# A written list of single operations, carried on to the end of token tile 1, and attention steps spread one at a time over tiles 2 and 3

## The chip, the cores and the metric

One Trainium2 chip, one core. The metric is the device time of one execution in microseconds (us). The kernel before took 558.62 us in the median of three runs (558.17 to 561.63).

## What is computed

The reference runs a chunked scan attention over 4 batches and 8 heads, 768 positions each, and feeds its output, 3072 tokens of 256 features, through two feed-forward networks:

```
for each chunk:                       # the kernel uses chunks of 96 positions, 8 of them
    cum = cumsum(log(clip(a)));  L = exp(cum_i - cum_j), causal
    y = ((C B^T) * L) x + exp(cum) * (C state)
    state = exp(sum) * state + sum_j B_j x_j exp(cum_end - cum_j)
h   = max(x w1, x w2, x w3)           # 256 -> 768
x   = h w_out                         # 768 -> 256
out = (sigmoid(x w_gate) * (x w_val)) w_out2      # 256 -> 1536 -> 256
```

All in float32. Products of the networks are made of three matmuls of split operands (high and low parts), and the weights arrive as 64-bit words that the kernel decodes to float32 and splits.

## The kernel before, in words

**Tiling.** The 3072 tokens are cut into six token tiles of 512. For a tile the first network has six slices m of 128 hidden features. A slice takes three groups of six matmuls (128x512) into three PSUM banks, one for each of w1, w2, w3; a copy and two maxima form the hidden slice s, a cast and a subtraction split it (hi, lo), and one group of six matmuls adds its share to the output banks. So a tile has 24 groups. The second network follows from about 281 us on.

**Attention.** It is cut into 64 steps; step k belongs to chunk c = k // 8 and to a group of four (batch, head) units. A step has a score (line 315, four products; float32 for steps 0 to 15, with masked C; later of bf16 parts, bi and cs), a weighting of the scores with the decay (weigh, line 337; matrix m), a small product for the states (states, line 331, on GpSimd) and an output product (outputs, line 348). After each four steps, high and low (lines 366, 370) write a split half chunk into the ring xt_hi, xt_lo, which the networks read, and turn (line 393) transposes the states for the next chunk. Decays come from a scan on VectorE (line 270), two for a pair of steps, in four buffers that load_decay (line 254) refills by DMA. For chunks from 2 on, B and C are loaded to one buffer bc, cast to bf16 three times with two subtractions between (parts 0, 1, 2), and scattered by 12 DMAs to bi and cs. Tile t needs the chunks that hold its tokens: tile 1 all steps below 24, tile 2 below 32, tile 3 below 44, tile 4 below 56.

**The list.** ORDER is a text of words, each one operation; in_order (line 674) emits them so that every engine, and each queue, runs its words in that order. The words that the text below uses:

- Ld, LB, LC, Lb, Lx, Lwa: loads of decays, of B and C for chunks 0 and 1, of bc for a later chunk, of x and states' inputs, of weight words.
- k: masked C (ScalarE). S, m, bx, y: score, weighting, states' product, output product of a step. D2a: a decay scan. H, X, T: high, low, turn of a half chunk.
- sg, raw, r (ScalarE), stt, add, hi, lo with a name such as a10: the decode of half a slice's weights. stt is a shift and an or.
- P, Q, Pd: cast, subtraction and scattering DMAs of a later chunk (P32: chunk 3, part 2).
- F, E, U, V, h, l, O: matmul group, copy, two maxima, cast, subtraction and output group of tile 0 (F21: slice 2, bank 1).
- I: idle products, matmuls whose result nobody reads; a bare I is 14 of them (IDLE0), I with a number is one.

ON_DVE names the words that run on VectorE instead of GpSimd. In the list before, F to O run over tile 0 and the steps go to 23 (SHARED); it ends with O4 on TensorE. From there on a loop (line 709) emits tiles 1 to 5, four slots for each slice, one after each of its three groups and one after the output group of the slice before. At the end of a slot, slot_end (line 699) starts attention steps until UNTIL's share for this slot is reached, and advances the generators: a step of tiles 2 and 3 is asked for its score in its slot, prepared (weighting, next decays, casts of the next chunk: prepare, line 402) two slots later and its output comes three slots later. In tiles 2 and 3 a loop of two starts steps in pairs. For k from SHARED on, even steps are weighted by a copy on ScalarE and a product on GpSimd (line 340), and the output products of four steps are issued together (line 352). The loop's instructions are put in order by a planner when the program is built; its position against the end of the list is not fixed by the list. After slice 0 of tile 4 the attention's memory is given up and the loads of the second network's weights follow (line 136); their decode starts with the eighth slot of that tile.

## Time and profile before

| | us |
|---|---|
| median of three runs | 558.62 |
| lowest, highest | 558.17, 561.63 |
| the profiled execution | 562.51 |
| its span, first to last instruction | 560.7 |
| TensorE busy in the span | 536.0 |
| VectorE, ScalarE, GpSimd busy | 389.1, 323.6, 114.9 |
| mean granted TensorE clock | 0.985 |

Engines are PE (TensorE matmul), PEld (its weight loads), DVE (VectorE), ACT (ScalarE), POOL (GpSimd) and SP (SyncE, which issues DMAs). Matmuls are pipelined: their listed duration (some 390 ns) is longer than the distance from one to the next, so the cost of a group is read from starts. Positions are us from the span's first instruction.

### The profile page before, as it was taken

How to read it: one execution, taken by the hardware profiler on the slowest of the kernel's cores; microseconds unless marked ns; L12 is line 12 of the kernel's file. 1: busy time of each engine (PE TensorE's matmuls, PEld its weight loads, DVE VectorE, ACT ScalarE, POOL GpSimd, SP SyncE). 2: the span in 40 equal slices, each digit the busy share in tenths (PEclk: the TensorE clock that was granted, in tenths of full speed). 3: DMA queues.
4: the chain of work that ended last, by engine and by line, in shares of the span. 5: the costliest groups of instructions: out<-in, count | busy, mean ns of one | idle time of the engine just before them, and what ended most of it. 6: DMA issues, size and time to landing. Idle time of an engine off the chain costs nothing.

```text
span 560.7 us, 7987 instructions
## 1 busy us (share of the span) xinstructions
PE 536.0 (96%) x2914; PEld 423.2 (75%) x2914; DVE 389.1 (69%) x656; ACT 323.6 (58%) x571; POOL 114.9 (20%) x153
## 2 busy tenths in 40 slices
...
PEclk9899998979999999999999999999999999999999
...
GB/s 220 294 355 137 211 127 287 154 189 149 158 204 113 91 1 321 54 1 145 60 97 0 1 1 2 0 1 75 1 0 2 0 2 75 1 0 1 0 1 76
DMA packets 33895, 50.53 MB, mean 90 GB/s; under 512 B 3392, under 2 KB 19904, under 8 KB 33856
## 3 DMA queue, kind: packets, MB, share of 16 engines
...
q8 instruction: 23, 0.38, 0.3%
q10 hardware_dynamic: 288, 0.39, 0.2%
q14 instruction: 16, 0.13, 0.1%
...
## 4 chain that ended last, share of the span: by engine, by line
PE 77%; DVE 9%; DMA 7%; ACT 2%; issue 2%; SPq 1%; POOL 1%; DVEq 0%; POOLq 0%; ACTq 0%
PE o L812 17%; PE uv L781 15%; PE ug L781 15%; PE u L428 7%; PE u L430 6%; PE u L429 6%; DMA dec<-ad 3%; DVE dec L273 3%; PE o L428 2%; PE o L429 2%; PE o L430 2%; PE y L355 2%; DMA cs<-parts 1%; PE s L322 1%; PE s L325 1%
## 5 line engine op out<-in xcount | busy, mean ns | idle before, releaser
L812 PE MATMUL o<-hi,w_d 128*128 128x512 f32 x288 | 97.6, 390 | 0.0
L428 PE MATMUL u<-xt_hi,w_a 128*128 128x512 f32 x216 | 88.5, 410 | 5.6 <-DVE s L510 2.2
L781 PE MATMUL ug<-xt_hi,w_g 128*128 128x512 f32 x252 | 91.5, 392 | 0.1
L781 PE MATMUL uv<-xt_hi,w_v 128*128 128x512 f32 x252 | 90.3, 390 | 0.0
L429 PE MATMUL u<-xt_lo,w_a 128*128 128x512 f32 x216 | 85.4, 395 | 0.0
L430 PE MATMUL u<-xt_hi,w_a 128*128 128x512 f32 x216 | 85.3, 395 | 0.0
L812 PEld LDWEIGHTS o<-hi,w_d 128*128 128x128 f32 x288 | 54.0, 188 | 11.3 <-ACT hi L855 0.2
L273 DVE TENSOR_TENSOR_SCAN dec<-dec,delta 128x388 f32<-128x388 f32 x64 | 58.5, 946 | 5.7 <-DMA dec<-ad 5.4
L856 DVE TENSOR_TENSOR lo<-y,hi 128x512 fp32r<-128x512 f32 x72 | 49.4, 687 | 16.5 <-ACT hi L855 15.6
L812 PE MATMUL o<-lo,w_d 128*128 128x512 f32 x144 | 56.4, 392 | 0.8 <-DVE lo L856 0.8
L781 PEld LDWEIGHTS ug<-xt_hi,w_g 128*128 128x128 f32 x252 | 47.3, 188 | 12.0 <-ACT ug L784 0.9
L781 PEld LDWEIGHTS uv<-xt_hi,w_v 128*128 128x128 f32 x252 | 47.3, 188 | 10.6 <-DVE y L852 0.8
L428 PEld LDWEIGHTS u<-xt_hi,w_a 128*128 128x128 f32 x216 | 41.3, 191 | 17.0 <-DVE s L510 2.4
L781 PE MATMUL ug<-xt_lo,w_g 128*128 128x512 f32 x126 | 49.1, 390 | 0.0
L781 PE MATMUL uv<-xt_lo,w_v 128*128 128x512 f32 x126 | 49.0, 389 | 0.0
L499 ACT CAST hi<-s 128x512 fp32r<-128x512 f32 x30 | 18.6, 620 | 52.1 <-DVE s L510 51.6
L430 PEld LDWEIGHTS u<-xt_hi,w_a 128*128 128x128 f32 x216 | 41.1, 190 | 9.1
L855 ACT CAST hi<-y 128x512 fp32r<-128x512 f32 x72 | 44.4, 619 | 5.7 <-DVE y L852 4.3
L429 PEld LDWEIGHTS u<-xt_lo,w_a 128*128 128x128 f32 x216 | 41.3, 191 | 7.9 <-DVE xt_lo L372 0.2
L852 DVE TENSOR_TENSOR y<-uv,y 128x512 f32<-128x512 f32 x36 | 24.7, 687 | 31.3 <-PE uv L781 31.2
L789 DVE TENSOR_TENSOR y<-ug,y 128x512 f32<-128x512 f32 x36 | 24.8, 689 | 24.4 <-ACT y L786 17.4
L786 ACT COPY sv<-uv 128x512 f32<-128x512 f32 x36 | 21.2, 588 | 33.5 <-PE uv L781 33.4
...
## 6 DMA issues: line engine op xcount, KB each, us to landing
...
```

What stands on the lines that cost most here:

```text
L273: dve.tensor_tensor_scan(out=f, data0=f, data1=delta.rearrange("p u w -> p (u w)"), initial=0.0, op0=ALU.mult, op1=ALU.add)
L428: pe.matmul(ps, wlo, a_hi(k), start=k == 0, stop=False)
L429: pe.matmul(ps, whi, a_lo(k), start=False, stop=False)
L430: pe.matmul(ps, whi, a_hi(k), start=False, stop=k == kn - 1)
L499: act.copy(hl[0], s)
L781: turn[0] = pe.matmul(ps, w, x, start=new and e == 0, stop=e == 2, skip_group_check=not new)
L786: evict[0] = act.copy(self.temp(1 if i == 6 else 2), ps)
L789: evict[1] = dve.tensor_tensor(out=self.t[k], in0=ps, in1=self.t[k], op=ALU.add)
L812: turn[0] = pe.matmul(acc2[t][d], w, x, start=n == 1 and e == 0, stop=n == M2 and e == 2)
L852: evict[1] = dve.tensor_tensor(out=g, in0=v, in1=g, op=ALU.mult)
L855: act.copy(hl[0], g)
L856: dve.tensor_tensor(out=hl[1], in0=g, in1=hl[0].bitcast(F32), op=ALU.subtract)
```

## The change

The list gets a new order from its first word on and goes on to the end of tile 1 (except that tile's last output group): F, E, U, V, h, l and O now carry slices 0 to b, where 6 to b are the slices of tile 1. Steps 24 to 31 are in it (LISTED = 32, which also takes the even ones among them back to VectorE), f0 is the copy of tile 0's output, and chunk 4's casts and scatters are in it. The loop starts with tile 2. UNTIL gives steps 32 to 47 to tile 2 and 48 to 63 to tile 3, over 23 slots instead of 19, and a step is started alone. The bare I, I13 and I14 are gone, and ON_DVE has other words. In the old list, lines are left out.

```diff
--- before.py
+++ after.py
@@ -42,37 +42,43 @@
 FIRST = 2 * NG
 MASKED = 8
 SHARED = 24
+LISTED = 32
 MTS = 8
 DECS = 4
-UNTIL = [12, 24, 36, 50, 64, 64, 64]
+UNTIL = [12, 24, 32, 48, 64, 64, 64]
 SLOT = {1: 0, 2: 1, 6: 3, 5: 4, 7: 6, 3: 2, 4: 5}
 WEIGHT = {1: 0, 2: 2, 3: 1, 4: 3, 5: 4, 6: 5, 7: 6}
 
 ORDER = """
-LB0 Lx00#0 I a clip Ld0 K delta I0 pk LC0 k3 k1 k4 clip0 Ld1 D0a astore k0 D0b S3 S0 k5 clip1 D1a
-D1b m3 k2 Lwa00#0 Lwa00 Lx00 bx1 LC1 S1 sga00 rawa00 stta00 bx2 ra00 I1 S4 k12 m0 Ld2 D2a Ld3 m1
-k7 m4 Lb2 S2 m2 I2 S5 S7 D2b D3a bx3 y3 D3b adda00 hia00 I3 I4 k10 P20 m5 k15 Lwa01#0 Lwa01 y2 bx0
-Ld4 y0 LB1 D4a m7 k6 S6 y1 Lx01#0 Lx01 D4b Q20 k9 S9 P21 Q21 k11 k8 m6 S8 m9 bx4 H00 S11 m8 X00
...
-X20 Pd30#3 Pd30#4 Pd30 U5 Pd32#0 Pd32 V5 Ld12 D12a Lx30#0 Lx30 h5 l5 O4 D12b Ld13 Lx40#0 Lx31#0
-Lx31 Ld14 Ld15 D13b T21 T20 D13a Lx40
+LB0 K Lwa00#0 a clip LC0 pk delta Lwa00 sga00 rawa00 stta00 Ld0 clip0 k6 Ld1 k2 k4 D0b S2 ra00 k5
+clip1 D1a m2 adda00 I0 astore hia00 Lb2 P20 k0 D0a k1 I1 I2 Lx00#0 Lx00 bx2 Q20 k3 D1b Ld2 D2b I3
+I4 I5 I6 LC1 S0 m0 S3 k7 bx3 m3 bx0 S1 m1 P21 Ld3 S5 m5 k9 I7 k8 D2a bx1 Lwa01#0 Lwa01 k13 k11 S7
+loa00 D3a D3b m7 Lx01#0 sga01 rawa01 S4 m4 S6 m6 y3 Q21 Lwa10#0 Lx01 bx4 stta01 ra01 y4 Ld4 D4a y0
+y2 y1 H00 X00 D4b I8 I9 Lwa10 bx7 sga10 rawa10 stta10 k14 I10 I11 LB1 I12 k10 adda01 Ld5 bx5 y5
+Lx10#0 Lx10 y7 bx6 y6 H01 Lwa11#0 Lwa11 D5b bx11 D5a S11 S10 m11 S9 ra10 S8 T00 bx10 m10 y11 y10
+adda10 Ld6 hia01 m9 bx9 y9 m8 hia10 bx8 y8 H10 Ld7 sga11 rawa11 X01 ra11 Lwa20#0 Lwa20 sga20 X10
+loa10 loa01 Lwa21#0 Lwa21 D7a rawa20 D6b S13 m13 F00 F01 stta11 adda11 E0 sga21 rawa21 U0 ra20
+Lwa30#0 Lwa30 stta20 stta21 Lx11#0 Lx11 F02 F10 hia11 loa11 ra21 k12 Lwa31#0 sga30 Lwa31 V0 F11
+F12 E1 D7b bx14 h0 adda20 bx15 S12 rawa30 U1 V1 Ld8 l0 hia20 Ld9 ra30 sga31 Lx20#0 Lx20 adda21
+stta30 D6a hia21 m12 Lwa41#0 loa20 rawa31 ra31 O0 stta31 loa21 Lwa40#0 Lwa40 adda30 hia30 F20
+loa30 adda31 F21 P22 k15 F22 T10 h1 D8a E2 U2 bx16 V2 Lwa41 sga41 Lwa50#0 Lwa50 sga40 S14 m14
+rawa40 ra40 stta40 l1 hia31 adda40 hia40 Pd21#0 S15 rawa41 loa31 F30 h2 bx12 E3 Pd22#0 Pd22 O1 T01
+bx13 D9a bx18 F31 Pd21#1 m15 y15 y13 Pd21#2 ra41 D8b bx17 sga50 l2 stta41 adda41 rawa50 ra50
+stta50 loa40 U3 hia41 y12 F32 O2 Pd20#0 Pd20#1 Pd20#2 Pd20#3 D9b V3 Pd20#4 F40 loa41 Pd20 E4 Pd21
+S19 m19 S17 m17 y14 Ld10 Lwa51#0 h3 S16 F41 m16 adda50 hia50 loa50 Lwa51 sga51 rawa51 D10a l3
+Lx21#0 Lx21 Ld11 Lx31#0 U4 S20 m20 ra51 F42 V4 h4 S18 m18 F50 E5 O3 S22 Lb3 stta51 S23 adda51
+hia51 bx19 y18 y16 D11a Ld12 D10b bx21 m22 loa51 y17 D11b m23 y19 H11 X11 F51 S21 P30 F52 l4 T11
+bx23 y23 Lx31 m21 bx22 H20 X20 y21 U5 bx20 y20 y22 H21 Lx30#0 X21 Q30 V5 h5 Lx30 Pd30#0 D12a bx24
+Lx41#0 Lx41 O4 D12b bx25 Pd30#1 Pd30#2 F60 T20 F61 P31 Q31 E6 U6 F62 V6 P32 l5 F70 E7 O5 f0 Pd30#3
+Ld13 Ld14 D13b D14a D13a F71 h6 F72 F80 l6 O6 U7 V7 F81 h7 l7 Pd30#4 Pd30 bx27 E8 Pd32#0 Pd31#0
+Pd31#1 Pd31#2 Pd31 Pd32 S27 m27 Lb4 U8 P40 F82 V8 S24 D14b Pd40#0 bx29 m24 Q40 F90 O7 h8 l8 F91
+S25 m25 E9 F92 U9 V9 S26 h9 l9 P41 Pd40#1 Pd40#2 Pd40#3 m26 O8 Ld15 D15a D15b bx26 Fa0 Ea S28 m28
+Fa1 S30 m30 bx30 Fa2 bx31 Pd40#4 Pd40 Ua Va Ld16 Ld17 Q41 P42 S29 m29 Fb0 Pd42#0 Pd42 S31 m31 T21
+Fb1 Eb Pd41#0 Pd41#1 Pd41#2 y27 Lx50#0 H30 X30 Ub bx28 y31 Fb2 Vb O9 Pd41 H31 X31 ha la Oa Lx40#0
+D17b Lx40 Ld18 D16b Ld19 hb T31 lb D16a Lx50 D17a T30
 """
 IDLE0 = 14
-ON_DVE = """loa10 loa11 adda21 adda30 adda31 adda41 Q30 l3""".split()
+ON_DVE = """Q20 loa10 adda20 adda21 loa21 adda40 l2 loa40 l5 l6 l7 l8""".split()
 
 
 class Pipe:
@@ -337,7 +343,7 @@
     def weigh(k):
 
         m, ps, dc = mt[k % MTS], scores.pop(k), factors(k)
-        if k >= SHARED and k % 2 == 0:
+        if k >= LISTED and k % 2 == 0:
             act.copy(m[:, :, 0:CH], ps[:, :, 0:CH])
             pool.tensor_tensor(out=m[:, :, 0:CH], in0=m[:, :, 0:CH], in1=dc[:, :, 1:LW],
                                op=ALU.mult)
@@ -441,8 +447,9 @@
         if m == mn - 1:
             pipe.add(finish(t, acc[t]))
 
-    def finish1(t, ps):
-        yield
+    def finish1(t, ps, wait=True):
+        if wait:
+            yield
         for d in range(KD):
             act.copy(y1[:, d, t * TT:(t + 1) * TT], ps[d])
 
@@ -588,30 +595,29 @@
                 wt1[m] = [(v[:, 0, b], v[:, 1, b]) for v in (wts[f"a{m}0"], wts[f"a{m}1"])
                           for b in range(4)]
 
-    def first_layer(kind, m, j):
+    def token_tile(kind, t, m, j):
 
         if kind == "F":
             if j == 0:
-                s = tmpp.tile([128, TT], F32, tag="s", bufs=3, name=f"s3_0_{m}")
-                hidden_of[m] = s, [tmpp.tile([128, TT], F32R, tag=h, name=f"{h}3_0_{m}")
-                                   for h in ("hi", "lo")]
-            banks_of[m, j] = ps = psu.tile([128, TT], F32, tag="up", name=f"u3_0_{m}_{j}")
-            w = wts[f"a{m}{j // 2}"]
+                s = tmpp.tile([128, TT], F32, tag="s", bufs=3, name=f"s3_{t}_{m}")
+                hidden_of[t, m] = s, [tmpp.tile([128, TT], F32R, tag=h, name=f"{h}3_{t}_{m}")
+                                      for h in ("hi", "lo")]
+            banks_of[t, m, j] = ps = psu.tile([128, TT], F32, tag="up", name=f"u3_{t}_{m}_{j}")
+            w, o = wts[f"a{m}{j // 2}"], t * TT
             three(ps, range(KD), KD, [(w[:, 0, b], w[:, 1, b]) for b in range(4)], lambda k: KD * (j % 2) + k,
-                  lambda k: xt_hi[:, k, 0:TT], lambda k: xt_lo[:, k, 0:TT])
+                  lambda k: xt_hi[:, k, o:o + TT], lambda k: xt_lo[:, k, o:o + TT])
             return
+        s, hl = hidden_of[t, m]
         if kind == "O":
-            down(0, m, M1, wt1[m], hidden_of[m][1], finish1)
-            return
-        s, hl = hidden_of[m]
-        if kind == "E":
-            evict[0] = act.copy(s, banks_of[m, 0])
+            down(t, m, M1, wt1[m], hl, lambda t, ps: iter(()))
+        elif kind == "E":
+            evict[0] = act.copy(s, banks_of[t, m, 0])
         elif kind in "UV":
-            evict[1] = dve.tensor_tensor(out=s, in0=banks_of[m, 1 + (kind == "V")], in1=s, op=ALU.max)
+            evict[1] = dve.tensor_tensor(out=s, in0=banks_of[t, m, 1 + (kind == "V")], in1=s, op=ALU.max)
         elif kind == "h":
             act.copy(hl[0], s)
         else:
-            (dve if f"l{m}" in ON_DVE else pool).tensor_tensor(
+            (dve if kind + "0123456789abcdef"[M1 * t + m] in ON_DVE else pool).tensor_tensor(
                 out=hl[1], in0=s, in1=hl[0].bitcast(F32), op=ALU.subtract)
 
     def clip(t):
@@ -638,6 +644,8 @@
             else:
                 (dve if word in ON_DVE else pool).tensor_tensor(out=r, in0=r, in1=parts[:, p],
                                                                 op=ALU.subtract)
+        elif word == "f0":
+            next(finish1(0, acc[0], False), None)
         elif word == "pk":
             sp.dma_start(out=pk, in_=pick)
         elif word == "a":
@@ -655,7 +663,7 @@
         elif word[:-3] in ("sg", "raw", "r", "stt", "add", "hi", "lo") and word[-3] == "a":
             weight(word[:-3], word[-3:])
         elif word[0] in "FOEUVhl":
-            first_layer(word[0], int(word[1]), int(word[2:] or 0))
+            token_tile(word[0], *divmod(int(word[1], 16), M1), int(word[2:] or 0))
         elif word[0] in "HXT":
             {"H": high, "X": low, "T": turn}[word[0]](int(word[1]), int(word[2]))
         else:
@@ -688,25 +696,25 @@
                 tails[i.engine] = i
 
     in_order(ORDER)
-    done[0] = SHARED
+    done[0] = LISTED
 
 
     slots = 4 * M1
-    slot = slots
+    slot = 2 * slots
     wp2, wq, hlp, psx = [], [], [], []
-    pend = (0, M1 - 1, M1, wt1[M1 - 1], hidden_of[M1 - 1][1], finish1)
+    pend = (1, M1 - 1, M1, wt1[M1 - 1], hidden_of[1, M1 - 1][1], finish1)
 
     def slot_end():
         t, s = divmod(slot, slots)
         if t + 1 < NTT:
-            goal = UNTIL[t] + (UNTIL[t + 1] - UNTIL[t]) * (s + 1) / (slots - 5)
+            goal = UNTIL[t] + (UNTIL[t + 1] - UNTIL[t]) * (s + 1) / (slots - 1)
             while done[0] < min(goal, UNTIL[t + 1]):
-                for _ in range(2 if t > 1 else 1):
+                for _ in range(1):
                     att_step(1 if t > 1 else 0)
         tick()
         weights_tick(t < NTT - 2 or s % 4 == 3)
 
-    for t in range(1, NTT):
+    for t in range(2, NTT):
         for m in range(M1):
             for hl in layer(t, m, wt1[m], 3, most):
                 slot_end()
```

## Rows read from the trace of the kernel before

**Rows 1.** The page, 40 slices of the span: the granted clock in tenths.
```profile
PEclk9899998979999999999999999999999999999999
```
**Rows 2.** Busy time by stretch: PE, PEld, DVE, ACT, POOL, then clock, DMA share, GB/s.
```profile
0.00:34.60 34.60, 27.90 (x229) 19.61 (x229) 21.88 (x36) 20.52 (x36) 15.82 (x35) 0.90 0.85 272
34.60:82.00 47.40, 42.87 (x294) 31.53 (x294) 45.34 (x70) 33.55 (x56) 29.70 (x31) 1.00 0.86 188
82.00:133.30 51.30, 44.20 (x289) 32.64 (x289) 32.36 (x58) 17.61 (x30) 25.24 (x32) 0.90 0.92 215
133.30:216.50 83.20, 81.69 (x626) 62.25 (x625) 54.80 (x91) 30.99 (x57) 42.81 (x54) 1.00 0.52 118
216.50:281.10 64.60, 64.60 (x287) 53.49 (x286) 51.29 (x103) 43.73 (x78) 1.29 (x1) 1.00 0.31 108
281.10:560.70 279.60, 274.75 (x1199) 223.73 (x1197) 183.44 (x302) 177.22 (x318) 0.00 (x0) 1.00 0.04 16
```
**Rows 3.** The chain that ended last, one piece: start, us, what.
```profile
283.95 1.36 PE ug L781 x6
```
**Rows 4.** Waits of PE, 82 to 133.3 us: in total, times, longest.
```profile
PE s L325 <- DMA dec<-ad: 4.1, 1, 4.1
PE u L428 <- DVE s L510: 2.2, 1, 2.2
```
**Rows 5.** Timeline of PE around step 32: start, us, instruction, idle time before it.
```profile
107.91 0.97 PE L355 MATMUL y<-mt,xs 128*32 128x112 f32 x30
113.01 0.48 PE L325 MATMUL s<-cs,bi 96*128 96x96 bf16 x4 [4.14 <-DMA dec<-ad]
```
**Rows 6.** Busy time by stretch, two stretches at the lower clock.
```profile
22.50:29.40 6.90, 6.80 (x28) 5.67 (x28) 5.67 (x13) 4.13 (x7) 4.03 (x8) 0.51 0.90 279
...
111.30:118.10 6.80, 5.09 (x16) 3.47 (x17) 1.53 (x4) 2.21 (x4) 2.84 (x2) 0.50 0.59 199
```
**Rows 7.** Timeline of PE: a lone score between groups; a y block and two scores.
```profile
104.70 0.48 PE L428 MATMUL u<-xt_hi,w_a 128*128 128x512 f32 x1
...
106.19 0.34 PE L325 MATMUL s<-cs,bi 96*128 96x96 bf16 x4
106.36 0.48 PE L428 MATMUL u<-xt_hi,w_a 128*128 128x512 f32 x1
...
163.99 0.97 PE L355 MATMUL y<-mt,xs 128*32 128x112 f32 x32
164.89 0.52 PE L325 MATMUL s<-cs,bi 96*128 96x96 bf16 x8
165.23 0.71 PE L428 MATMUL o<-hi,w_a 128*128 128x512 f32 x2
```
**Rows 8.** Groups of DVE, 34.6 to 82 us: busy us, mean ns, idle before.
```profile
L576 DVE SCALAR_TENSOR_TENSOR t_a<-raw_a,sg 128x512 int32<-128x512 int32 x10 | 8.9, 887 | 0.2 <-ACT raw_a L570 0.2
...
L579 DVE CUSTOM_DVE_ANT_0 r_a<-t_a,r_a 128x1024 uint16<-128x1024 uint16 x4 | 3.1, 788 | 0.1
L585 DVE TENSOR_TENSOR w_a<-r_a,w_a 128x512 fp32r<-128x512 f32 x2 | 2.5, 1229 | 0.0
...
L639 DVE TENSOR_TENSOR bc<-bc,parts 128x896 f32<-128x896 f32 x1 | 1.2, 1183 | 0.0
```
**Rows 9.** Timeline of ACT: the last cast of chunk 4's B and C.
```profile
103.73 0.94 ACT L296 CAST parts<-bc 128x896 bf16<-128x896 f32 x1 [1.15 <-POOL bc L300]
```
**Rows 10.** Timeline of PE in the start: idle products and scores.
```profile
1.78 4.99 PE L670 MATMUL idle<-sg 128*128 128x512 bf16 x14 [1.78 <-POOL sg L156]
...
10.44 2.02 PE L322 MATMUL s<-y 128*128 128x96 f32 x16 [0.39 <-ACT y L311]
...
22.60 5.41 PE L322 MATMUL s<-y 128*128 128x96 f32 x24 [1.03 <-DMA y<-in_bch]
```
**Rows 11.** Timeline of SP's queue: decay load 4, and the second network's first weights.
```profile
16.24 0.33 SPq L257 DMA_DIRECT2D dec<-ad  x1
...
211.07 0.38 SPq L136 DMA_DIRECT2D raw_g<-in_wg  x1
```

More of the change, by code (lines that the diff above doesn't have):

```diff
@@ L51 @@
 ORDER = """
-LB0 Lx00#0 I a clip Ld0 K delta I0 pk LC0 k3 k1 k4 clip0 Ld1 D0a astore k0 D0b S3 S0 k5 clip1 D1a
-D1b m3 k2 Lwa00#0 Lwa00 Lx00 bx1 LC1 S1 sga00 rawa00 stta00 bx2 ra00 I1 S4 k12 m0 Ld2 D2a Ld3 m1
-k7 m4 Lb2 S2 m2 I2 S5 S7 D2b D3a bx3 y3 D3b adda00 hia00 I3 I4 k10 P20 m5 k15 Lwa01#0 Lwa01 y2 bx0
-Ld4 y0 LB1 D4a m7 k6 S6 y1 Lx01#0 Lx01 D4b Q20 k9 S9 P21 Q21 k11 k8 m6 S8 m9 bx4 H00 S11 m8 X00
-sga01 rawa01 stta01 ra01 Lx10#0 bx6 Lx10 T00 bx7 Lwa11#0 bx5 bx9 I5 I6 adda01 I7 I8 k14 y4 y7 Ld5
@@ L57 @@
-I9 I10 I11 D5b m11 y6 bx8 P22 hia01 I12 Lwa11 sga11 I13 k13 Ld6 D5a S10 m10 bx11 bx10 y8 y5 H01 y9
-y11 X01 y10 H10 X10 Lwa10#0 Lwa10 D6a sga10 rawa10 Ld7 loa00 ra10 rawa11 ra11 loa01 stta10 D7b S15
-m15 F00 F01 E0 Lwa20#0 Lwa20 sga20 U0 Lwa21#0 Lwa21 S13 adda10 hia10 stta11 adda11 loa10 rawa20
-ra20 stta20 D6b m13 F02 Ld8 V0 sga21 hia11 rawa21 stta21 F10 E1 F11 Lwa30#0 Lwa30 I14 Ld9 adda20
-hia20 loa11 h0 sga30 rawa30 F12 U1 S12 loa20 F20 Lwa31#0 Lx11#0 Lx11 bx15 D9a stta30 l0 ra21
-adda21 ra30 adda30 m12 O0 hia21 loa21 Lwa41#0 bx13 V1 bx12 D7a Lwa31 hia30 sga31 rawa31 stta31
@@ L69 @@
-Pd30#0 m18 D11a O3 F50 E5 bx21 S22 y18 stta51 S20 adda51 m22 S23 F51 D11b Pd31#0 Pd31#1 hia51 y16
-bx23 T11 Pd30#1 P32 y21 Pd30#2 bx22 y22 Pd31#2 m23 loa51 y23 l4 y19 m20 y20 H21 X21 H20 F52 Pd31
-X20 Pd30#3 Pd30#4 Pd30 U5 Pd32#0 Pd32 V5 Ld12 D12a Lx30#0 Lx30 h5 l5 O4 D12b Ld13 Lx40#0 Lx31#0
-Lx31 Ld14 Ld15 D13b T21 T20 D13a Lx40
+LB0 K Lwa00#0 a clip LC0 pk delta Lwa00 sga00 rawa00 stta00 Ld0 clip0 k6 Ld1 k2 k4 D0b S2 ra00 k5
+clip1 D1a m2 adda00 I0 astore hia00 Lb2 P20 k0 D0a k1 I1 I2 Lx00#0 Lx00 bx2 Q20 k3 D1b Ld2 D2b I3
@@ new lines @@
+I4 I5 I6 LC1 S0 m0 S3 k7 bx3 m3 bx0 S1 m1 P21 Ld3 S5 m5 k9 I7 k8 D2a bx1 Lwa01#0 Lwa01 k13 k11 S7
+loa00 D3a D3b m7 Lx01#0 sga01 rawa01 S4 m4 S6 m6 y3 Q21 Lwa10#0 Lx01 bx4 stta01 ra01 y4 Ld4 D4a y0
+y2 y1 H00 X00 D4b I8 I9 Lwa10 bx7 sga10 rawa10 stta10 k14 I10 I11 LB1 I12 k10 adda01 Ld5 bx5 y5
+Lx10#0 Lx10 y7 bx6 y6 H01 Lwa11#0 Lwa11 D5b bx11 D5a S11 S10 m11 S9 ra10 S8 T00 bx10 m10 y11 y10
+adda10 Ld6 hia01 m9 bx9 y9 m8 hia10 bx8 y8 H10 Ld7 sga11 rawa11 X01 ra11 Lwa20#0 Lwa20 sga20 X10
+loa10 loa01 Lwa21#0 Lwa21 D7a rawa20 D6b S13 m13 F00 F01 stta11 adda11 E0 sga21 rawa21 U0 ra20
```

22 lines of the change are left out of this document (16 added, 6 removed).

## The prediction

> **What bounds the kernel now.** I read the page first, then the stages, then the waits of the slow stage. The slices show TensorE (PE) at 9 of 10 from slice 9 on, with dips before that, and the granted clock below 1.00 in four groups of slices, all in the first 120 us [rows 1]. The table by stage puts limits to this [rows 2]. From 216.5 us to the end PE is busy for all but 4.8 of 344 us at clock 1.00: nothing in that part can give much, and anything that brings its start forward brings the end forward by as much. What can be won lies in the first 216 us, which fall into four stretches. I cut them by the matmuls of the list: the start up to F00 (34.6 us), the list's token tile 0 up to the end of O4 (82.0), the loop's tile 1 up to the end of O4 of that tile (133.3), and tiles 2 and 3 (216.5).
>
> A group of six 128x512 matmuls costs 1.36 us when nothing stands between them [rows 3]. A tile has 24 such groups, 32.6 us. Tile 1 took 51.3 us for them and 12 attention steps, with 44.2 us of PE busy and a mean clock of 0.90 [rows 2]. The waits there name two holes of 4.1 and 2.2 us [rows 4]. The first is the score of step 32: PE stood from the y block at 107.91 to 113.01 [rows 5]. The row names a decay load, but a score reads only bi and cs, so I put it down to the last scattered parts of chunk 4, issued just ahead of that load on the same queue. Behind the hole the clock fell: from 111.3 to 118.1 us it was 0.50 [rows 6], the 1.2 GHz level, and the 5.1 us of work from 113.0 to 118.1 gave away half, 2.5 us. So one such late score costs 4.1 + 2.5 = 6.6 us. The second hole is a max on VectorE (DVE) queued behind scans and transposes.
>
> In tile 0 the picture differs: DVE is busy 45.3 of 47.4 us [rows 2]. That stretch is DVE's, not PE's.
>
> **Tile 1 in the list.** After the change, tile 1 has its 24 groups (F60 to Fb2, O5 to Oa) in a hand-ordered row, and eight steps (24 to 31) with it, where it had twelve. No score of chunk 4 is left in it: S32 now comes with tile 2. In the list P42, the last cast of chunk 4, stands six groups, two y blocks and a score ahead of S32. The price of a lone score: from one group's start at 104.70 to the next at 106.36 are 1.66 us, 0.30 more than 1.36 [rows 3, 7]. A y block of four steps took 0.90 us, 163.99 to 164.89 [rows 7], about 1.04 with the same 0.13 us that a group after an interruption takes longer. Sum: 24 x 1.36 + 8 x 0.30 + 2 x 1.04 = 37.1 us, and 0.9 us that I allow for small waits: 38.0 against 51.3, **13.3 us less**. Bounds: no wait at all gives 14.2 less; both old holes with their clock, 8.8 more, gives 5.4 less.
>
> DVE can bear it. The even steps 24 to 30 now multiply scores on DVE (about 0.5 us each) instead of ScalarE and GpSimd (POOL), and l5 to l8 move to DVE; but in 82.0 to 133.3 DVE was busy only 32.4 of 51.3 us [rows 2], so some 6 us more find room.
>
> **Tile 0 in its new order.** PE's groups there are the same; DVE sets the length, so I count what DVE runs between X10 and V5. Scans (12), score products (12), maxima (12) and transposes (three sets) stay. It loses one shift-or of 0.89 us (stta10 goes ahead of F00), one of four weight additions (0.79) and Q30 (1.18), and gains one w_a subtraction (1.23) [rows 8]; the single l stays (l2 for l3). Sum: **1.6 us less**. The other orders I cost at nothing since DVE has no idle time to be closed beyond 2.1 us. Bounds: those means hold outliers (the shift-or's mean of 0.89 comes from runs of 0.68 and some near 1.8), so I allow 5 less if these vanish, and 3 more if the new order meets as many waits as it has unknown edges.
>
> **The start.** The 14 idle products that open the queue go (and I13, I14), and weight a00 is loaded and decoded first. On ScalarE (ACT) that puts its decode and P20, the first cast of chunk 2, ahead of masks k0, k1, k3, k7. P20's load is now issued before decay loads 2 and 3, so it should be there in time. By ACT's queue (three decode steps, three masks, a fourth mask, the hi cast, P20) S0 comes at about 15.5 us, where S0 and S1 ran from 10.44 [rows 10]. Behind S0 stand m0 and m1, which free the buffer that decay load 4 needs: its issue at 16.24 [rows 11] goes to about 19.3, and LB1, queued behind it on SP, goes with it. So scans and scores of chunk 1 start some 3 us later. DVE was busy for only 21.9 of the first 34.6 us [rows 2], waiting for scores between its scans, so I let it take up two of the three. F00 comes **1.0 us later**; bounds: 1.5 earlier (the weight's decode, now out of the way, is all gain) and 5.6 later (below).
>
> Removing the idle products changes the clock's history. The 14 took 4.99 us [rows 10], 0.36 each, where a matmul of as many columns takes 0.23 at full clock (1.36 / 6, [rows 3]): the first of them ran at the lower level. Three scores in the stretch at 0.51 took 5.41 us, two at full clock 2.02 [rows 6, 10]: a score costs 0.8 us more at 1.2 GHz. In the new list S2 and seven idle products run back to back ahead of S0, so I expect the upper level by S0. Beside this stands the Trainium skill ("TensorE: Matmul & The Clock Gate", "Part 1: The HAM clock gate"): throttled is the default, and only sustained activity lifts it. By that rule the scores behind S0 could still run throttled, and the sum would be -2.3 us instead of -6.9; it is the second rival, whose price below comes from rows. By the rows, the old list's fillers did lift the clock, so the trace agrees with the rule as far as it goes.
>
> **Tiles 2 and 3.** They now take 32 steps instead of 28, singly. Two scores together take 0.34 us, 164.89 to 165.23 [rows 7], and 0.13 behind them: 0.47 against 0.60 for two lone ones, 14 x 0.13 = 1.8 us. Four more steps are 4 x 0.30 + 1.04 = 2.2. **4.0 us more.** Then the even pace. Chunk 5's last cast P2 comes with step 35's preparation, about slot 6 of tile 2, and S40 is asked for at slot 11: five slots of 83.2 / 48 = 1.73 us [rows 2], 8.7 us. In the old tile 1, cast at 103.73 to score at 113.01 were 9.3 us [rows 5, 9]. So S40, and S56 likewise in tile 3, come a little late: I take 1.5 us each, **3.0**, bounds 0 and 13.2 (6.6 each). S48 has seven slots and is free of this.
>
> The attention's last y block slips from before tile 4 into its first slots. The first load of the second network's weights waits for it: it was issued at 211.07 [rows 11], 5.4 us before tile 4, and would come about 2.5 us into it. The decode starts after the eighth slot, 8 x 1.36 = 10.9 us in, so a load that lands within 8 us costs nothing. Without that cover ACT would stall on it, and with it the maxima and PE.
>
> **Sum**: -13.3 - 1.6 + 1.0 + 4.0 + 3.0 = **-6.9 us**. The profiled execution took 562.5 us with a span of 560.7, so it would give 555.6. It lies 3.9 us above the median of the three timed runs, 558.6; taken from that, **551.7 us**.
>
> **Rivals.**
> *More is won* (the new tile 0 loses 5 and S40, S56 are ready): 6.4 better, 545.3. For: DVE's outliers are there to be lost. Against: DVE is full in both orders.
> *A cold start*: were the seven scores S0 to S6 all at 1.2 GHz and passed on whole, F00 would come 5.6 us later instead of 1.0: 556.3. Seven scores at 0.8 are those 5.6. For: 22.5 to 29.4 us ran at 0.51 even with the fillers [rows 6]. Against: the dense run of S2 and I0 to I6.
> *One or two chunk boundaries as bad as S32 was*: with one at 6.6, 556.8; with both, 561.9.
> *Slower*: S48 too, so three boundaries at 6.6 instead of 3.0 in all: 568.5. It decides once the way from P2's cast to the next chunk's first score exceeds the slots between them by some 4 us. For: 9.3 against 8.7 us at two of them, and PE stood at S32 from 108.9 on. Against: in 133.3 to 216.5, with two such boundaries, PE was idle for only 1.5 of 83.2 us [rows 2].
> *The order does not hold*: the end of the list may be overtaken by the loop's instructions; then tile 1 keeps its holes, and the rest is about even: 558.6.
>
> **How the numbers follow.** Likeliest, 0.52: 551.7, own range 547.5 to 555.5, four fifths of it under 553.0. More won 0.13, cold start 0.12, one or two boundaries 0.09, order lost 0.04, three boundaries 0.10. Faster by over 1% (about what a measurement of this kernel can tell from no change) is under 553.0: 0.42 + 0.13 = 0.55. Within 1%: 0.10 + 0.12 + 0.09 + 0.04 = 0.35. Slower: 0.10. The range 545.0 to 562.0 leaves out three boundaries and half of "more won".
>
> **What would show it.** Right: tile 1's 24 groups within 37 to 40 us, no hole over 1 us and clock 1.00 in it; F00 at 34 to 37 us and O4's end at 79 to 84; tiles 2 and 3 at 86 to 92; the stretch from tile 4 on unchanged near 344 us. Wrong: a PE wait of 3 us or more at the scores of steps 32, 40 or 56 with clock 0.50 behind it; F00 past 38 us; O4 past 86, which would mean that the new order starves DVE; or waits of ACT for the second network's weights in tile 4.

## The result and the profile after

The changed kernel took 553.98 us (median of four runs, 552.49 to 554.9) where the kernel before, run beside it, took 558.96: a ratio of 0.9894 [0.9859, 0.9929]. Timed again later, beside other kernels, it took 554.14 us against 560.80, a ratio of 0.987 [0.9837, 0.9902]. So it is faster by 1.1 to 1.3%, some 5.0 to 6.7 us. 551.7 us had been forecast.

The profiled execution took 554.9 us with a span of 553.1. By stretch, cut at F00, at the first group of each tile and at the start of tile 4, and in the last row of the second fence the one stretch at half clock (columns: PE, PEld, DVE, ACT, POOL busy, then clock, DMA share, GB/s). The first fence is the row of clocks of the page.

```profile
PEclk9899999999999999999999999999999999999999
```
```profile
0.00:35.20 35.20, 22.35 (x213) 18.08 (x214) 24.02 (x38) 20.45 (x36) 15.20 (x35) 0.95 0.78 251
35.20:79.40 44.20, 42.11 (x293) 31.23 (x293) 42.27 (x68) 31.41 (x54) 29.22 (x30) 1.00 0.81 215
79.40:122.30 42.90, 38.31 (x248) 29.45 (x247) 29.83 (x52) 14.48 (x23) 11.99 (x15) 1.00 0.79 162
122.30:207.90 85.60, 83.02 (x636) 61.48 (x635) 60.69 (x103) 33.23 (x59) 49.64 (x65) 1.00 0.71 145
207.90:273.60 65.70, 65.70 (x319) 54.12 (x318) 53.13 (x105) 44.54 (x80) 1.27 (x1) 1.00 0.37 128
...
20.00:23.40 3.40, 3.40 (x17) 3.30 (x17) 2.81 (x5) 2.61 (x5) 2.20 (x3) 0.50 0.89 217
```

Set beside [rows 2], the start is 0.6 us longer, tile 0 is 3.2 us shorter, tile 1 8.4 us shorter, tiles 2 and 3 are 2.4 us longer and tile 4's stretch is 1.1 us longer (the last y block, 32 matmuls, has moved into it: x319 for x287). The sum is 7.6 us, from a span of 560.7 to 553.1. [rows 1] has three slices below 9 (not four groups, as I had read it); one is left. The record of the clock begins with its first rise, 5.5 us into the profile of before and 13.1 into this one; what ran ahead of that counts as full in these rows and in the mean clocks below.

The waits of PE in tile 1, and then in tiles 2 and 3 (total, times, longest), answer [rows 4]:

```profile
PE s L331 <- DMA cs<-parts: 2.6, 1, 2.6
PE s L331 <- DMA bc<-in_bch: 0.8, 1, 0.8
PE o L435 <- DVE lo L620: 0.7, 1, 0.7
...
PE s L331 <- DMA bc<-in_bch: 1.1, 1, 1.1
PE u L434 <- DVE s L517: 0.8, 2, 0.4
PE s L331 <- DVE s L517: 0.7, 1, 0.7
```

With one of 0.5 us that is left out, they come to 4.6 us in tile 1 and 2.6 in tiles 2 and 3. So a hole at step 32 is left, at 120.41. Its chain can be read across four engines (timelines of POOL, ACT, SP's queue and PE: start, us, instruction, idle time before it):

```profile
107.92 1.91 POOL L645 TENSOR_TENSOR bc<-bc,parts 128x896 f32<-128x896 f32 x1
...
104.14 0.93 ACT L643 CAST parts<-bc 128x896 bf16<-128x896 f32 x1
...
109.86 0.94 ACT L643 CAST parts<-bc 128x896 bf16<-128x896 f32 x1 [3.45 <-POOL bc L645]
...
110.83 0.56 SPq L638 DMA_DIRECT2D bi<-parts  x1
...
114.02 0.59 SPq L270 DMA_DIRECT2D xs<-in_xh  x1
114.66 0.55 SPq L638 DMA_DIRECT2D cs<-parts  x1
...
117.46 0.39 PE L434 MATMUL u<-xt_hi,w_a 128*128 128x512 f32 x1
120.41 0.33 PE L331 MATMUL s<-cs,bi 96*128 96x96 bf16 x4 [2.56 <-DMA cs<-parts]
120.56 0.71 PE L434 MATMUL o<-hi,w_a 128*128 128x512 f32 x2
```

The subtraction Q41 ran on POOL at 107.92, the last cast P42 at 109.86, and the last scattered part was issued at 114.66, behind five other scatters and a load of xs; the score came 5.7 us after that issue. By the list's order the first two of the six scatters (Pd42) carry part 2 and the last four (Pd41) carry part 1, which P41 had cast at 104.14: they stood on the queue behind Pd42, which waited for P42. So the part that came last had been cast over 9 us before its last scatter was issued; no run put Pd41 ahead of Pd42. From cast to score it is 10.6 us, where the old tile 1 had 9.3 [rows 5, 9]. Unlike in [rows 6], no half clock follows the hole.

**How much of the gain is the clock.** The profiled execution of before, at a mean clock of 0.985, was one of its slower ones. Over 71 timed runs of the kernel before, its mean clock was 0.990 and its mean span 558.8 us; over ten runs of the changed one, 0.9976 and 552.1. Since half clock is one of two levels, 0.010 and 0.0024 below full mean 11.3 and 2.7 us at half clock in an execution, 8.6 us less, of which up to half, 4.3 us, is work not done. The kernel before alone gives a smaller slope: its 15 runs at 0.985 and 0.986 have a mean span of 560.2 us, its six at 0.997 have 556.2, 4.0 us for 0.011 of the clock, and by that slope the 0.0077 between the two kernels are worth 2.7 us. At a clock of 0.997 the changed kernel's two runs have 552.4. So of a mean gain of 6.7 us in span some 3.8 to 4.0 are there at one clock, and the rest is time at half clock that the changed kernel has more rarely. That is argued from clocks and spans of whole runs; no run held the clock fixed.

### The profile page after: what moved, and what is told of

It is laid out like the page before. It is cut to its first block, busy times and chain, and to the rows that moved or that the text cites. A ratio compares the mean times of both kernels' runs of the same rounds, so it can differ in the third digit from the quotient of the medians.

```text
span 553.1 us, 7932 instructions
## 1 busy us (share of the span) xinstructions
PE 526.1 (95%) x2897; PEld 418.1 (76%) x2898; DVE 393.4 (71%) x664; ACT 321.3 (58%) x567; POOL 107.3 (19%) x145
## 4 chain that ended last, share of the span: by engine, by line
PE 71%; DMA 10%; DVE 9%; issue 3%; ACT 3%; SPq 2%; POOL 1%; DVEq 0%; ACTq 0%; POOLq 0%
PE o L820 17%; PE ug L789 15%; PE uv L789 15%; PE u L434 6%; PE u L435 5%; PE u L436 5%; DVE dec L279 3%; DMA dec<-ad 3%; DMA cs<-parts 3%; PE o L435 2%; PE o L434 2%; PE o L436 2%; DMA bc<-in_bch 2%; PE y L361 2%; SPq L638 1%
## 5 line engine op out<-in xcount | busy, mean ns | idle before, releaser
L820 PEld LDWEIGHTS o<-hi,w_d 128*128 128x128 f32 x288 | 54.0, 188 | 11.3 <-ACT hi L863 0.2
L789 PEld LDWEIGHTS ug<-xt_hi,w_g 128*128 128x128 f32 x252 | 47.3, 188 | 12.0 <-ACT ug L792 0.9
L789 PEld LDWEIGHTS uv<-xt_hi,w_v 128*128 128x128 f32 x252 | 47.3, 188 | 10.6 <-DVE y L860 0.8
L434 PEld LDWEIGHTS u<-xt_hi,w_a 128*128 128x128 f32 x216 | 40.6, 188 | 14.1 <-issue 1.7
L863 ACT CAST hi<-y 128x512 fp32r<-128x512 f32 x72 | 44.4, 619 | 5.8 <-DVE y L860 4.3
L436 PEld LDWEIGHTS u<-xt_hi,w_a 128*128 128x128 f32 x216 | 40.6, 188 | 8.8
L351 DVE TENSOR_TENSOR mt<-s,dec 128x384 f32<-128x384 f32 x48 | 25.8, 550 | 12.0 <-PE s L331 10.5
```

Source lines behind the costliest of these rows:

```text
L351: last[0] = dve.tensor_tensor(out=m[:, :, 0:CH], in0=ps[:, :, 0:CH], in1=dc[:, :, 1:LW], op=ALU.mult)
L434: pe.matmul(ps, wlo, a_hi(k), start=k == 0, stop=False)
L436: pe.matmul(ps, whi, a_hi(k), start=False, stop=k == kn - 1)
L789: turn[0] = pe.matmul(ps, w, x, start=new and e == 0, stop=e == 2, skip_group_check=not new)
L820: turn[0] = pe.matmul(acc2[t][d], w, x, start=n == 1 and e == 0, stop=n == M2 and e == 2)
L863: act.copy(hl[0], g)
```

## The experiments

My theory: the gain is tile 1's, from the two holes and the half clock behind them, and tile 0's shorter queue on DVE adds a little; lone scores in tiles 2 and 3 cost some of it. The rivals: the gain comes from the four steps moved out of tile 1, whatever the list's order; or from the even pace; or from the new tile 0.

The table that follows has each kernel's stretches from its one profile (first group of a tile to the first of a later one, us) and its timing against the kernel before on the same chip. The kernel before was timed beside each, and medians of different rows come from several sessions, so it is the ratios that can be compared. after_again is the changed kernel a second time:

> The changed kernel itself, timed once more beside the next three on the same chip: ratio 0.987 to 0.992 against the kernel before, its first timing gave 0.9894.

| kernel | tile 0 | tiles 1+2 | tile 3 | tile 4 on | median us | ratio |
|---|---|---|---|---|---|---|
| before | 47.2 | 92.1 | 42.5 | 344.3 | 558.96 to 560.80 | 1 |
| changed | 44.2 | 85.3 | 43.2 | 345.3 | 553.98 | 0.9894 [0.9859, 0.9929] |
| after_again | 44.3 | 84.4 | 43.1 | 345.3 | 554.14 | 0.987 [0.9837, 0.9902] |
| t0_new | 44.3 | 94.9 | 42.5 | 344.1 | 562.48 | 1.0028 [1.0003, 1.0053] |
| t1_new | 47.2 | 82.6 | 43.2 | 345.2 | 553.99 | 0.9886 [0.9843, 0.9929] |
| old_even | 47.2 | 85.9 | 43.1 | 345.3 | 555.62 | 0.9923 [0.9897, 0.9949] |
| old_shares | 47.3 | 88.6 | 44.3 | 344.3 | 560.68 | 1.0003 [0.998, 1.0026] |
| old_pace | 47.2 | 92.3 | 41.4 | 345.3 | 561.42 | 1.0022 [0.9998, 1.0046] |
| new_pairs | 44.3 | 88.0 | 44.3 | 344.2 | 557.41 | 0.9953 [0.9926, 0.998] |
| pairs_24 | 44.2 | 87.1 | 43.8 | 344.3 | 556.27 | 0.9912 [0.9884, 0.994] |
| singles_19 | 44.2 | 90.2 | 44.4 | 345.1 | 557.88 | 0.9955 [0.9931, 0.998] |
| q41_early | 44.2 | 85.0 | 43.1 | 345.3 | 553.45 | 0.9868 [0.9842, 0.9893] |
| t1_q41 | 47.2 | 84.3 | 43.2 | 345.3 | 555.53 | 0.9904 [0.988, 0.9929] |
| q41_idle | 44.2 | 86.9 | 43.1 | 345.3 | 553.71 | 0.9869 [0.9828, 0.9911] |

### The new order of tile 0 alone, and of tile 1 alone

t0_new is the changed list up to O4 and the words behind it that prepare chunk 3, in their new order; then the old loop:

```diff
-LISTED = 32
+LISTED = 24
-UNTIL = [12, 24, 32, 48, 64, 64, 64]
+UNTIL = [12, 24, 36, 50, 64, 64, 64]
...
-            goal = UNTIL[t] + (UNTIL[t + 1] - UNTIL[t]) * (s + 1) / (slots - 1)
+            goal = UNTIL[t] + (UNTIL[t + 1] - UNTIL[t]) * (s + 1) / (slots - 5)
-                for _ in range(1):
+                for _ in range(2 if t > 1 else 1):
-    for t in range(2, NTT):
+    for t in range(1, NTT):
...
 (the list ends, behind O4)
+Pd30#0 D12b Pd30#1 Pd30#2 T20 P31 Q31 P32 l5 Pd30#3 Ld13 Ld14 D13b D13a Pd30#4 Pd32#0 Pd31#0
+Pd31#1 Pd31#2 Pd31 Pd32 Ld15 T21 Lx40#0 Lx40
```

> The new list up to O4 (tile 0 alone in its new order, with what the old list held of chunk 3 behind it), then the old loop for tile 1 with the old shares and pairs. My theory (the gain is tile 1's): the start and tile 0 bring some 2.5 us, tile 1 takes 50 us or more again with a late score of step 32; ratio to before 0.995 to 1.000. Rival (the gain is the new order of the start and of tile 0): ratio 0.987 to 0.991, as the whole change.

It was no faster: 1.0028, above both ranges. Tile 0 gave its 3 us. Behind it, the waits of PE in the stretch of tile 1, and that stretch by busy time:

```profile
PE s L326 <- DMA cs<-parts: 8.9, 1, 8.9
PE o L430 <- DVE lo L615: 2.9, 1, 2.9
```
```profile
79.20:133.40 54.20, 42.39 (x290) 31.69 (x289) 34.11 (x59) 19.16 (x32) 25.71 (x32) 0.87 0.92 182
```

The first score of chunk 3 stood for 8.9 us at 94.24, with 13.7 us at half clock. The new order casts chunk 3's parts late, since in it that chunk's first score stands ten groups into tile 1; the old loop asks for it after two. So this kernel doesn't price tile 0's order by itself; it shows that the order is only good together with the tile 1 that follows it.

t1_new is the opposite: the old list up to O4, then the changed list's words of tile 1 (without those that prepare chunk 3, which the old words have done by then) and the changed loop. Against the changed kernel:

```diff
 (the list, around O4)
+F52 Pd31 X20 Pd30#3 Pd30#4 Pd30 U5 Pd32#0 Pd32 V5 Ld12 D12a Lx30#0 Lx30 h5 l5 O4 Lx31#0 Lx31 bx24
+Lx41#0 Lx41 D12b bx25 F60 T20 F61 E6 U6 F62 V6 F70 E7 O5 f0 Ld13 Ld14 D13b D14a D13a F71 h6 F72
...
-ON_DVE = """Q20 loa10 adda20 adda21 loa21 adda40 l2 loa40 l5 l6 l7 l8""".split()
+ON_DVE = """loa10 loa11 adda21 adda30 adda31 adda41 Q30 l3 l5 l6 l7 l8""".split()
```

> The old list up to O4, then the new list's words for tile 1 and steps 24 to 31, then the new loop (steps 32 to 63 one at a time). My theory: F00 and O4 as before (34.6 and 82 us), tile 1 within 40 to 43 us, tiles 2 and 3 some 3 us longer than before; ratio 0.988 to 0.993, most of the whole change. Rival (the gain is tile 0's order): ratio 0.998 or above.

0.9886, the whole gain. The new order of tile 0 and of the start is not needed for it.

### The list as it was, the rest as changed

old_even keeps the old list and its end, and changes only how the loop hands out steps.

```diff
-UNTIL = [12, 24, 36, 50, 64, 64, 64]
+UNTIL = [12, 24, 32, 48, 64, 64, 64]
-            goal = UNTIL[t] + (UNTIL[t + 1] - UNTIL[t]) * (s + 1) / (slots - 5)
+            goal = UNTIL[t] + (UNTIL[t + 1] - UNTIL[t]) * (s + 1) / (slots - (5 if t == 1 else 1))
-                for _ in range(2 if t > 1 else 1):
+                for _ in range(1):
```

> The kernel before with the new shares alone: 8 steps in tile 1, 16 each in tiles 2 and 3, one at a time; no new list. Rival (moving the scores of chunk 4 out of tile 1 is all that counts): the 4.1 us hole and the low clock behind it go, ratio 0.988 to 0.992. My theory: the hole goes but the scans still stand before tile 1's maxima and the lone steps cost 4 us in tiles 2 and 3; ratio 0.994 to 1.000.

0.9923, some three fifths to three quarters of the gain, from three changed lines. That lies at the edge of the rival's range and under mine. Tile 1 without any written list, its waits, and the waits of tiles 2 and 3:

```profile
81.30:123.80 42.50, 39.13 (x242) 30.27 (x241) 26.73 (x47) 13.65 (x24) 18.44 (x24) 0.96 0.74 189
```
```profile
PE s L325 <- DVE s L510: 2.3, 1, 2.3
PE s L325 <- DMA cs<-parts: 1.0, 1, 1.0
...
PE u L428 <- DVE s L510: 2.9, 4, 1.7
```

42.5 us for tile 1, as long as the written one (42.9 with its hole at step 32). The hole at step 32 is gone here; the older one, a maximum queued on DVE, stays, with 3.4 us at half clock.

### Shares alone, pace alone

old_shares makes only the first edit of the diff above (pairs and 19 slots stay), old_pace only the other two.

> The kernel before with one line changed: 32, 48 and 64 steps are due by the end of tiles 1, 2 and 3, in place of 36, 50 and 64. The list, the steps in pairs and the due slots (counted to 19) stay. If moving four steps out of tile 1 is what gains, tile 1's holes before the first scores of chunk 4 go and the time falls by some 4 us against the kernel before, ratio 0.990 to 0.995. If the even single pace is needed with it, the pairs of the sixteen steps in tiles 2 and 3 cost back what new_pairs showed against the changed kernel (3.4 us), and the ratio is 0.997 to 1.001.

> The kernel before with the steps of tiles 2 and 3 one at a time and spread over all 24 slots (still 36, 50, 64 steps, the list as it was). If the pace alone gains, the waits behind pairs go in tiles 2 and 3 and the time falls by 2 to 4 us against the kernel before, ratio 0.993 to 0.997, with the first scores of chunk 4 still late in tile 1. If it gains only beside the moved steps, the ratio is 0.999 to 1.002. My prediction's term for lone scores (0.9 us for each of 14 steps less 0.62) would make it up to 4 us slower, ratio 1.002 to 1.007.

Neither gains: 1.0003 and 1.0022. Waits of PE in tile 1, of old_shares and then of old_pace:

```profile
PE s L325 <- DVE s L510: 2.3, 1, 2.3
...
```
```profile
PE s L325 <- DMA dec<-ad: 3.9, 1, 3.9
...
```

With the shares alone, the late score of step 32 goes from tile 1; with the pace alone it stays. By stretch, old_shares' tile 1, tile 2 and tile 3, then old_pace's tile 1 and tiles 2 and 3:

```profile
80.80:121.70 40.90, 37.64 (x242) 29.15 (x242) 26.70 (x47) 13.66 (x24) 18.46 (x24) 1.00 0.77 196
121.70:169.50 47.80, 43.59 (x338) 33.13 (x337) 34.64 (x57) 18.32 (x33) 27.27 (x34) 0.96 0.85 175
169.50:213.80 44.30, 41.70 (x337) 31.91 (x336) 27.59 (x45) 16.37 (x31) 22.11 (x28) 1.00 0.48 100
```
```profile
80.60:131.20 50.60, 43.51 (x290) 32.16 (x289) 32.53 (x58) 17.59 (x30) 25.17 (x32) 0.93 0.93 206
131.20:214.20 83.00, 81.55 (x593) 60.91 (x592) 52.69 (x88) 30.70 (x55) 42.70 (x54) 1.00 0.51 108
```

The shares win 10.4 us in tile 1 and lose 8.9 in tiles 2 and 3 (92.1 for 83.2). old_even's tiles 2 and 3 took 86.5 with the same 32 steps. With 28 steps the pace changes nothing (83.0 for 83.2). So the pace is worth 5.6 us in these profiles, but only once each of the two tiles holds 16 steps. In old_shares' tiles 2 and 3 PE's waits come to 6.7 us, 3.7 of them for a maximum, against old_even's 2.9; with half of the 3.4 us at half clock behind the longest of them, that is 5.5 of the 5.6 us.

### Which half of the pace

new_pairs undoes both lines of the pace in the changed kernel, pairs_24 and singles_19 one each.

```diff
 new_pairs: both; singles_19: the first pair of lines; pairs_24: the second
-            goal = UNTIL[t] + (UNTIL[t + 1] - UNTIL[t]) * (s + 1) / (slots - 1)
+            goal = UNTIL[t] + (UNTIL[t + 1] - UNTIL[t]) * (s + 1) / (slots - 5)
-                for _ in range(1):
+                for _ in range(2 if t > 1 else 1):
```

> The changed kernel with steps 32 to 63 started in pairs over 19 slots again (still 16 a tile). By my term for lone scores (0.13 us for each pair split, 16 pairs) it is 2 us faster than the changed kernel: ratio to before 0.985 to 0.987. Rival (the even pace is what keeps tiles 2 and 3 free of waits): scores of steps 40 to 48 wait for their parts, ratio 0.992 or above.

> The changed kernel with the other half undone: steps in pairs, spread over all 24 slots. If pairs were the cost it keeps most of new_pairs' 3.4 us, ratio 0.993 to 0.996, with waits of the first layer's products for the maximum (2 us at the longest in new_pairs). If the packed slots were the cost, it equals the changed kernel, ratio 0.988 to 0.991. My prediction's price of lone scores would make it 2 to 4 us faster than the changed kernel, ratio 0.982 to 0.986.

> The changed kernel with one number changed: the steps of tiles 2 and 3 are due by slot 19 again, still one at a time. new_pairs undid both halves of the pace and cost 3.4 us. If pairs were the cost (the maxima queued behind two steps' products and scans), this costs little: 0 to 1 us over the changed kernel, ratio 0.988 to 0.992. If the packed slots were the cost, it is some 2 to 3.4 us slower than the changed one, ratio 0.993 to 0.996, with waits of scores for parts or first factors in tiles 2 and 3.

All three are slower than the changed kernel: by 3.7 us (singles_19, 557.88 for 554.14, intervals apart), by 2.1 us (pairs_24: the intervals overlap; its eight runs lie at 554.6 to 558.4 us, the changed kernel's six beside them at 552.2 to 555.2), and new_pairs by 0.0059 to 0.0083 of the ratio, 3.3 to 4.6 us. My prediction has the pairs' price with the other sign (its term was 1.8 us for 14 pairs; the 4 us in two of the expectations overstate it). Of the two halves the packing weighs, by the medians, at least as much as the pairs, and they overlap: both together cost no more than the packing alone. Waits of PE in tiles 2 and 3, singles_19 first, then pairs_24, then a pair in pairs_24 (timeline of PE):

```profile
PE u L434 <- DVE s L517: 3.1, 1, 3.1
PE u L434 <- ACT mt L347: 2.1, 2, 1.3
PE s L331 <- DMA dec<-ad: 2.0, 2, 1.7
PE s L331 <- ACT mt L347: 1.2, 1, 1.2
...
```
```profile
PE u L434 <- DVE s L517: 2.2, 2, 1.8
PE o L434 <- ACT hi L506: 1.1, 3, 0.4
PE s L331 <- DVE s L517: 1.1, 3, 0.4
...
```
```profile
136.15 0.33 PE L331 MATMUL s<-cs,bi 96*128 96x96 bf16 x4 [0.36 <-DVE s L517]
136.86 0.73 PE L434 MATMUL o<-hi,w_a 128*128 128x512 f32 x2 [0.38 <-ACT hi L506]
```

With the steps packed into 19 slots, PE waits 8.6 us in tiles 2 and 3, 3.3 for maxima and 5.3 for ACT's copies and, by the profile, decay loads. Which queue is behind each of these I did not separate. A pair that should save 0.13 us on PE stands 0.36 us for the maximum ahead of its second score, and the output group behind it 0.38 for a cast. Three of the sixteen pairs do so, 2.2 us in all, as much as sixteen pairs would save (16 x 0.13 = 2.1); such a pair of short waits also stands in the trace of before, at 149.20 and 149.91, and I had not counted it.

### The hole that is left, and the idle products

q41_early puts two words of the changed list earlier, t1_q41 the same two in t1_new; q41_idle is q41_early with the fourteen idle products.

```diff
-S25 m25 E9 F92 U9 V9 S26 h9 l9 P41 Pd40#1 Pd40#2 Pd40#3 m26 O8 Ld15 D15a D15b bx26 Fa0 Ea S28 m28
-Fa1 S30 m30 bx30 Fa2 bx31 Pd40#4 Pd40 Ua Va Ld16 Ld17 Q41 P42 S29 m29 Fb0 Pd42#0 Pd42 S31 m31 T21
+S25 m25 E9 F92 U9 V9 S26 h9 l9 P41 Q41 Pd40#1 Pd40#2 Pd40#3 m26 O8 Ld15 D15a D15b bx26 Fa0 Ea
+P42 S28 m28 Fa1 S30 m30 bx30 Fa2 bx31 Pd40#4 Pd40 Ua Va Ld16 Ld17 S29 m29 Fb0 Pd42#0 Pd42 S31
+m31 T21
 (q41_idle also)
-LB0 K Lwa00#0 a clip LC0 pk delta Lwa00 sga00 rawa00 stta00 Ld0 clip0 k6 Ld1 k2 k4 D0b S2 ra00 k5
+LB0 I K Lwa00#0 a clip LC0 pk delta Lwa00 sga00 rawa00 stta00 Ld0 clip0 k6 Ld1 k2 k4 D0b S2 ra00 k5
```

> The changed kernel with two words of its list put earlier: Q41 right behind P41, P42 right behind Ea, so that the subtraction of chunk 4's second part stands ahead of two broadcasts on GpSimd and the third cast ahead of S28. If the 2.56 us that the scores of step 32 waited at 120.41 for the loaded parts are on the path, that wait falls under 1 us and the kernel is about 2 us faster than the changed one (ratio against the kernel before 0.983 to 0.988, where the changed kernel has 0.989). If the wait only moves to the next operation that is late (a scan behind the later broadcasts, the split of the next input), the ratio stays at 0.988 to 0.992.

> t1_new (the old order through tile 0, the new one behind it) with Q41 and P42 put earlier in the same way. t1_new's own wait of step 32 was 1.43 us, so at most some 1.4 us are to be had: ratio 0.985 to 0.989 where t1_new had 0.9886. If it equals q41_early, the new order of tile 0 brings nothing here either.

> q41_early with the fourteen idle products put back at the head of the list. The changed kernel's first products on TensorE come at half clock until 13.1 us of its span. If the missing idle products cost what my prediction took (1.0 us at the start), F00 comes about 1 us earlier than q41_early's 33.88 and the ratio is 0.984 to 0.987. If the idle products only fill time in which the chip waits for loads anyway, F00 stays at 33 to 35 and the ratio stays at q41_early's 0.987.

The wait at step 32 went from 2.56 to 0.33 us in q41_early, but only to 1.66 in q41_idle, and in t1_q41 it was 1.59 where t1_new had 1.43. The wait at step 35, 0.7 us in the changed kernel and in t1_new, grew in all three, to 1.94, 1.75 and 1.59. The wait at step 40, 1.1 and 1.3 us there, was gone in q41_early and grew to 3.0 and 2.0 in the other two. Step 35 in q41_early, then step 40 in q41_idle (timelines of PE):

```profile
127.50 0.33 PE L331 MATMUL s<-cs,bi 96*128 96x96 bf16 x4 [1.94 <-DVE s L517]
```
```profile
142.17 0.47 PE L331 MATMUL s<-cs,bi 96*128 96x96 bf16 x4 [3.00 <-DMA xs<-in_xh]
```

0.9868 and 0.9869 cannot be told from the changed kernel's 0.987 and 0.9894, and t1_q41 at 0.9904 not from t1_new: what the two words win at step 32, where they win anything, is in good part lost at later steps. No version I ran beats the changed kernel by more than its interval. The idle products did not show the 1.0 us that I had put on them: q41_idle spent 9.1 to 15.9 us at half clock, and F00 came at 33.63 where q41_early had 33.88, less of a difference than between profiles of one start (below).

Whether the new order of tile 0 is worth anything stays open. Its 3 us are in every profile that has it, but t1_new, without them, is as fast as the changed kernel, having lost less in tiles 1 and 2 (82.6 us for 84.4 and 85.3); of q41_early and t1_q41, on one chip, the one with them is 2.1 us faster; the intervals of their ratios overlap, but their runs do not (553.1 to 554.0 and 554.8 to 556.5).

## Why the prediction was right, and where its terms were off

The sign held, and 553.98 lies within the likeliest case's own range. The sum of -6.9 us stands against -7.6 in the profiles, but in timed runs the gain was 5.0 to 6.7. That the sum came so near is luck: tile 1 was 4.9 us worse than forecast, tiles 2 and 3 were 4.6 better (3.5 with what slipped into tile 4) and tile 0 some 1.5 better.

**The start: +1.0 forecast, +0.6.** S0 was put at 15.5 us and ran at 14.53, and decay load 4's issue at 19.76 for 19.3. In the start, PE's timeline shows what the clock did:

```profile
9.27 2.02 PE L328 MATMUL s<-y 128*128 128x96 f32 x8 [9.27 <-ACT y L317]
11.09 2.69 PE L678 MATMUL idle<-delta_s 128*128 128x512 bf16 x7
14.53 3.04 PE L328 MATMUL s<-y 128*128 128x96 f32 x24 [0.75 <-ACT y L317]
19.29 1.43 PE L328 MATMUL s<-y 128*128 128x96 f32 x8 [1.72 <-DVE mt L351]
```

S2 ran at half clock (8 matmuls in 2.02 us), the seven products behind it brought the full one, and three scores then took 3.04 us. Other profiles say how far one may trust the 0.6: F00 came at 33.7 to 35.2 us in the seven that share this start, and at 32.8 to 34.6 in the six with the old one. "The upper level by S0" was right, and the cold start was not the case; what I had not seen is that the clock fell once more, from 20.0 to 23.4, behind the 1.72 us for which S5 waited.

**Tile 0: -1.6 forecast, -3.0 to -3.2.** DVE is busy nearly throughout in both orders (42.27 us of 44.20 here), and its busy time fell by 3.1 us, as much as the stretch, so the method held. Its groups there:

```profile
L583 DVE SCALAR_TENSOR_TENSOR t_a<-raw_a,sg 128x512 int32<-128x512 int32 x9 | 8.0, 902 | 0.0
...
L592 DVE TENSOR_TENSOR w_a<-r_a,w_a 128x512 fp32r<-128x512 f32 x3 | 3.1, 1046 | 0.0
L586 DVE CUSTOM_DVE_ANT_0 r_a<-t_a,r_a 128x1024 uint16<-128x1024 uint16 x3 | 2.4, 789 | 0.1
...
L620 DVE TENSOR_TENSOR lo<-s,hi 128x512 fp32r<-128x512 f32 x1 | 0.7, 667 | 0.0
```

Against [rows 8], the shift-ors lose 0.9 us, r_a 0.7 and Q30 1.2, as forecast. The one l lost 1.1 more (0.67 us where its like in the old list took 1.78), and the third w_a subtraction cost 0.6 for 1.23. The failed step is "the single l stays": it stayed, but not its outlier.

**Tile 1: -13.3 forecast, -8.4.** This is the largest miss. Its own signs failed: 42.9 us for 37 to 40, and a hole of 2.56 us for none over 1. Waits of 4.6 us stand where I had allowed 0.9, and the failed step is the sentence on P42 "six groups, two y blocks and a score ahead of S32": I had taken PE's work from cast to score for cover, without laying out the way between, which takes 10.6 us here and took the 9.3 us in the old trace that I then did use for S40. By the prediction's prices the six groups, the blocks and the score are 10.5 us (the list has a second score there, S29), which would have covered nearly all of it. But S32 came back into tile 1: the planner put a matmul of tile 2 at 117.46 and then the step's score ahead of tile 1's fifth O group, Oa. So only four of the six groups ran ahead of it, 8.0 us from the cast to the end of the work at 117.85; the other two, less that matmul, are 2.5 us, as long as the wait. No run kept S32 behind them. That the half clock would go from tile 1 was right in this profile, and the mean clocks of all ten runs, 0.996 and above, leave room for little more than one stretch of 3.4 us in any of them.

**Tiles 2 and 3: +7.0 forecast, +2.4, or +3.5 with the y block that slipped into tile 4.** Two terms failed. Lone scores were to cost 1.8 us: undoing them (pairs_24) made the time 2.1 us longer, not shorter, though by intervals that overlap; with 28 steps (old_pace) the timing, 0.1 us faster to 2.6 slower, neither shows nor excludes the 1.8. S40 and S56 were to wait 1.5 us each: counted in scores from step 32, S40 stood 1.11 us at 143.74, S56 not at all. Also, the +2.2 for four steps counted four whole steps, while S32's score fell into tile 1 and the last y block into tile 4.

**Tile 4.** The loads of the second network were issued at 210.38, 2.5 us into tile 4 as forecast, and ACT waited no longer than 0.2 us on a decode there: the cover held.

**Rivals.** The list's order held up to its last group on TensorE, Oa, which S32 overtook. One boundary did wait, S32 for 2.56 and S40 for 1.11 us, but without the half clock that made 6.6 us of it in the old tile 1. The reason I gave for the gain was right in place (tile 1, the hole at step 32) and wrong in means: the written list isn't what removes it. Moving four steps out of tile 1 does, and the even pace keeps tiles 2 and 3 from giving it back; old_shares, old_pace and old_even show that. What the written list adds to this is, by the differences between old_even and the three timings that have it, between 0.3 and 0.5% of the time; the intervals of some of these pairs overlap. Without the even pace it is as much: new_pairs has 0.9953 where old_shares, the same shares and pace on the old list, has 1.0003, with intervals that just touch. Which part of the list brings it is not shown.
